# Transposing x of the first problem in ten tiles of 128 tokens instead of four blocks of 320

## The chip, the cores and the metric

The kernel runs on one core of a Trainium2 chip, as one program that drives five engines: TensorE (PE: matmuls; PEld: the weight loads that go with them), VectorE (DVE), ScalarE (ACT), GpSimd (POOL) and SyncE (SP). SP and ACT issue DMAs, each on a queue of its own. The metric is the device time of one execution in microseconds. Before the change the median of five runs is 696.78 us (695.6 to 711.94).

## The reference, cut to what matters

Two problems, A and B, of the same shapes, each a grouped-query attention over a cache, with a projection ahead of it and one behind:

```python
B, Sq, D = 16, 80, 576
Hq, Hkv, Sk, Dh = 32, 16, 512, 128
q = (lambda x, *d: x.transpose(*d))((x @ wq).reshape(B, Sq, Hq, Dh), 0, 2, 1, 3)
k = jnp.repeat(k_cache, rep, axis=1)
v = jnp.repeat(v_cache, rep, axis=1)
scores = jnp.einsum("bhqd,bhkd->bhqk", q, k) * (Dh ** -0.5)
p = _softmax(scores, axis=-1)
o = jnp.einsum("bhqk,bhkd->bhqd", p, v)
return (lambda x, *d: x.transpose(*d))(o, 0, 2, 1, 3).reshape(B, Sq, Hq * Dh) @ wo
```

The results of A and B stand side by side in the last dimension. All tensors are bf16. x of one problem is 16 x 80 = 1280 tokens of 576 values.

## The kernel before, in words

**Units.** The work is cut into 128 units U (problem, group of four K/V heads, batch entry): 64 for A, then 64 for B. A unit has K and V of four heads (512 KB each), its scores (L894: 16 matmuls over 160 columns, two query heads of 80 tokens together), exponentials on ScalarE (L899, three matmuls at a time), and the product with V (L991, L1007). Four units of neighbouring batch entries make a window W with one division by the row sums on VectorE (L1026, L1031), and eight make one output projection (L1050 transposes, L1087 matmuls, L1099 to L1109 sums).

**Queries.** For four batch entries (320 tokens, a block) and eight query heads, a step m of L850 makes q^T: eight jobs `qp` of five matmuls each (L867), one for each 128-row chunk of the 576 rows of x^T and Wq. The fifth chunk takes the last 128 columns of x and meets a Wq chunk whose upper 64 rows are zero. The result is copied to `qT` (L874, by VectorE, or ScalarE for every other head of m = 0). Steps m = 0 to 3 use blocks 0 to 3 of A.

**x^T.** A matmul needs x with its features on the partitions. For B the transposing DMA does that (L773, L776). For A, x is loaded as it lies into the unused accumulator `acc`, and TensorE transposes it (L798) against an identity. Each block of 320 tokens has two loads, of 256 and of 64 tokens (L782, L785), and 15 transposes: for each of the five chunks two of 128 tokens and one of 64. They are put into PSUM in three parts (two chunks, two chunks, one) and copied to `xT` and `xR` (L804: the second part by ScalarE, the others by VectorE). Blocks 0 to 3 use acc rows 2 to 9. The K of units 0 to 3 is also loaded as it lies and transposed on TensorE (L951, L959, L964); from U = 4 on, K comes by the transposing DMA (L927) into five buffers `kT`. K of units 2 and 3 is loaded into acc rows 2 to 5, so its loads wait for the transposes of x blocks 0 and 1 (in the program, after their projections' place in the order). V is loaded (L931) into three buffers and copied by GpSimd into five others with a column of ones beside each head (L934).

**Order.** Every operation is added with an engine and a key; `_Sched.finalize` sorts by key, derives the waits from named resources that are read and written, and each engine runs its operations in that order. Nothing is reordered at run time. The keys are written out by hand in tables: `X_T` for the loads of x, `TX_T` for its transposes (-98, -89, -63, -12), `K_T` and `V_T` for K and V, `W1_T` for the second Wq, `WO_T` for the first Wo, `Q_T` for the early projections; m = 0 stands at -96 + 2i. Jobs on TensorE that go through PSUM take three banks in turn (`JB`, L1134), and the copies that follow them are placed by `place_followers` behind their job's modelled end.

In that order, TensorE begins with eight warm-up matmuls (L752), then the transposes of block 0, four projections, the transposes of block 1 (in front of the fifth projection of m = 0), four projections, the transposes of block 2, and then projections of m = 1 and 2 mixed with the K transposes of unit 0. Scores begin at 31.93 us, and the transposes of block 3 follow the first three of them, at 32.14 us.

**Queues.** SP's queue begins with x of block 0 (two loads), block 2 (two), block 1 (two), V0, K0, K1, V1, x of block 3 (two), K2, V2, K3, V3, and then the transposing K loads with the V loads between them. ACT's queue begins with the first Wq, in three pieces of 256, 256 and 512 columns, each as a load of 512 rows (L822) and one of the last 64 rows (L825), then Wo (L843) and the second Wq (L833).

Of the kernel before, what the change touches and what calls it, by code (L numbers as in the profile page):

```python
# [7 lines left out]
BF16 = mybir.dt.bfloat16  # L8
# [11 lines left out]
NX = 5  # L20
# [598 lines left out]
def bass_concat_heads__gqa_block_cached__gqa_block_cached__near_ridge_kernel(  # L619
# [9 lines left out]
    B, SQ, D = A_x.shape  # L629
# [6 lines left out]
    NSU = 2 * NOCT * B  # L636
    NW = NSU // 4
# [4 lines left out]
    DC = D // 2  # L642
    QN = 4 * SQ
    PVB = (3, 4)
    OKS = 7 % NX
    X_T = (-801.0, -800.0, -800.9, -791.7)
    K_T = (-798.0, -794.0, -60.0, -40.0, 0.0, 3.5, 35.0, 35.5, 59.0, 67.5)
    KVP = (-56.0, -41.0)
    NVS = 20
# [15 lines left out]
    sb = lambda name, shape, dt: fast.enter_context(nc.sbuf_tensor(name, shape, dt))  # L665
    ident = sb("ident", [128, 128], BF16)
    ones = sb("ones", [128, 128], BF16)
    xT = sb("xT", [128, NX, 4, QN], BF16)
    xR = sb("xR", [128, NX, QN], BF16)
    wq_sb = sb("wq_sb", [128, 2, 5, 1024], BF16)  # L670
    qT = sb("qT", [128, NQ, 4, 4, 160], BF16)
    kT = sb("kT", [128, NK, 4, 512], BF16)
# [7 lines left out]
    osb = sb("osb", [128, NOSB, D], BF16)  # L680
    acc = sb("acc", [128, 10, D], F32)
    rinv = sb("rinv", [128, 5 * NSU], F32)
    okm = xT[:, OKS, 0:2, :].rearrange("p a b -> p (a b)")
    warm = acc[:, 0, 0:256].bitcast(BF16)
    okn = sb("okn", [128, 3], F32)
    okb = sb("okb", [128, 1], BF16)
    ps = fast.enter_context(nc.psum_tensor("ps", [128, 8, 512], F32))
    psb = ps[:].bitcast(BF16)
    sem_names = (["e_pe", "e_act", "e_dve", "e_pool"]
                 + ["d_wi%d" % i for i in range(3)] + ["d_wo%d" % i for i in range(2)] + ["d_wq%d" % i for i in range(2)]  # L690
                 + ["d_x%d" % i for i in range(NX)] + ["d_out%d" % i for i in range(NOSB)]
                 + ["d_k%d" % i for i in range(NK)] + ["d_v%d" % i for i in range(NV)])
    sems = {n: nc.alloc_semaphore("f_" + n) for n in sem_names}
# [3 lines left out]
    def R(res, ver):  # L697
        return (res, ver)
# [65 lines left out]
    add("pe", -890, em_warm, reads=[R(("ones",), 0), R(("acc", 0, 0), "warm")], writes=[R(("ps", 0), ("W",))], name="warm")  # L764
    IDENT = R(("ident",), 0)

    for xb in range(8):
        prob, c = divmod(xb, 4)
        x_ap = probs[prob][0].rearrange("b s d -> (b s) d")[c * QN:(c + 1) * QN, :]
        sl = xb % NX  # L770

        def em_ldx(e, x_ap=x_ap, sl=sl):
            return e.dma_start_transpose(xT[:, sl, 0:4, :], x_ap[:, 0:512].rearrange("n (c d) -> n c d", d=128))  # L773

        def em_ldx2(e, x_ap=x_ap, sl=sl):
            return e.dma_start_transpose(xR[:, sl, :], x_ap[:, D - 128:D])  # L776

        if prob == 0:
            xin = acc[:, 2 + 2 * c:4 + 2 * c, :].rearrange("p a d -> p (a d)").bitcast(BF16).rearrange("p (a d) -> p a d", d=D)

            def em_ldz(e, x_ap=x_ap, xin=xin):
                return e.dma_start(xin[:, 0:2, :], x_ap[0:256, :].rearrange("(a p) d -> p a d", p=128))  # L782

            def em_ldzb(e, x_ap=x_ap, xin=xin):
                return e.dma_start(xin[0:64, 2, :], x_ap[256:QN, :])  # L785

            for k_, em in ((0, em_ldz), (1, em_ldzb)):
                add("sp", X_T[c] + 0.1 * k_, em, writes=[R(("acc", 2 + 2 * c + k_, h_), ("x", xb)) for h_ in range(2)],
                    dsem="d_x%d" % sl, name="ldz%d%s" % (xb, "ab"[k_]))
            for part, (k0, k1) in enumerate(((0, 2), (2, 4), (4, 5))):  # L790
                def em_tx(e, bank, k0=k0, k1=k1, xin=xin):
                    last = None
                    for ck in range(k0, k1):
                        d0 = 128 * ck if ck < 4 else D - 128
                        for a in range(3):
                            n = 128 if a < 2 else 64
                            c0 = QN * (ck - k0) + 128 * a
                            last = e.transpose(psb[:, bank, c0:c0 + n], xin[0:n, a, d0:d0 + 128], ident[0:n, 0:n])  # L798
                    return last

                def em_txev(e, bank, k0=k0, k1=k1, sl=sl, part=part):
                    src = psb[:, bank, 0:QN * (k1 - k0)]
                    dst = xT[:, sl, k0:k1, :].rearrange("p a b -> p (a b)") if k0 < 4 else xR[:, sl, :]
                    return e.copy(dst, src) if part == 1 else e.tensor_copy(dst, src)  # L804

                job(TX_T[c] + 0.3 * part, em_tx,
                    [R(("acc", 2 + 2 * c + k_, h_), ("x", xb)) for k_ in range(2) for h_ in range(2)] + [IDENT],
                    "tx%d.%d" % (xb, part), ("X", xb, part),
                    [("act" if part == 1 else "dve", 0.0, em_txev, [], [R(("xT", sl, part), xb)], None)])
            continue  # L810
        t = 16.0 * (36, 46.5, 50, 54)[c] + 9.0
        add("sp", t, em_ldx, writes=[R(("xT", sl, k_), xb) for k_ in range(2)], dsem="d_x%d" % sl, name="ldx%d" % xb)
        add("sp", t + 0.1, em_ldx2, writes=[R(("xT", sl, 2), xb)], dsem="d_x%d" % sl, name="ldx%db" % xb)

    for goct in range(2 * NOCT):
        prob, q = divmod(goct, NOCT)
        wq_ap, wo_ap = probs[prob][3][:, q * 1024:(q + 1) * 1024], probs[prob][4][q * 1024:(q + 1) * 1024, :]
        sl = goct % 2
        if goct == 0:
            for hf, (n0, n1) in enumerate(WQ0):  # L820
                def em_a(e, wq_ap=wq_ap, n0=n0, n1=n1):
                    return e.dma_start(wq_sb[:, 0, 0:4, n0:n1], wq_ap[0:512, n0:n1].rearrange("(c p) n -> p c n", p=128))  # L822

                def em_b(e, wq_ap=wq_ap, n0=n0, n1=n1):
                    return e.dma_start(wq_sb[64:128, 0, 4, n0:n1], wq_ap[512:576, n0:n1])  # L825

                add("act", -799.6 + 0.2 * hf, em_a, writes=[R(("wq", 0, hf, "a"), 0)], dsem="d_wi%d" % hf, name="ldwa0.%d" % hf)
                add("act", -799.5 + 0.2 * hf, em_b, writes=[R(("wq", 0, hf, "b"), 0)], dsem="d_wi%d" % hf, name="ldwb0.%d" % hf)
        else:
            for ck in range(5):  # L830
                def em_w(e, wq_ap=wq_ap, sl=sl, ck=ck):
                    if ck < 4:
                        return e.dma_start(wq_sb[:, sl, ck, :], wq_ap[128 * ck:128 * ck + 128, :])  # L833
                    return e.dma_start(wq_sb[64:128, sl, 4, :], wq_ap[512:576, :])

                wr = [R(("wq", sl, ck), goct)]
                if goct == 2:
                    wr += [R(("wq", 0, hf, ab), 1) for hf in range(3) for ab in "ab"] if ck == 0 else []
                add("act" if goct < 2 else "sp", 256.0 * (goct - 1) + 16.0 + 20.0 * ck if goct > 1 else W1_T[ck], em_w,
                    writes=wr, dsem="d_wq%d" % sl, name="ldw%d.%d" % (goct, ck))  # L840
        for pc in range(4):
            def em_wo(e, wo_ap=wo_ap, sl=sl, pc=pc):
                return e.dma_start(wo_sb[:, sl, 2 * pc:2 * pc + 2, :],  # L843
                                   wo_ap[256 * pc:256 * pc + 256, :].rearrange("(h p) n -> p h n", p=128))

            t = 256.0 * goct - 56.0 + 22.0 * pc
            add("sp" if goct else "act", t if goct else WO_T[pc], em_wo, writes=[R(("wo", sl, pc), goct)], dsem="d_wo%d" % sl,
                name="ldwo%d.%d" % (goct, pc))

    for m in range(2 * NOCT * 4):  # L850
# [4 lines left out]
        for i in range(8):  # L855
# [8 lines left out]
            def em_qp(e, bank, i=i, wsl=wsl, xsl=xsl):  # L864
                last = None
                for ck in range(5):
                    last = e.matmul(ps[:, bank, 0:QN], lhsT=wq_sb[:, wsl, ck, i * 128:(i + 1) * 128],  # L867
                                    rhs=xT[:, xsl, ck, :] if ck < 4 else xR[:, xsl, :], start=(ck == 0), stop=(ck == 4))
                return last

            def em_qev(e, bank, g=g, s_=s_, qsl=qsl, ev=ev):
# [2 lines left out]
                return e.copy(dst, src) if ev == "act" else e.tensor_copy(dst, src)  # L874

            if goct == 0:
                rd = [R(("wq", 0, (0, 0, 1, 1, 2, 2, 2, 2)[i], ab), 0) for ab in "ab"]
            else:
                rd = [R(("wq", wsl, ck), goct) for ck in range(5)]
            job(t, em_qp, rd + [R(("wqz",), 0)] + [R(("xT", xsl, k_), xb) for k_ in range(3)],  # L880
                "qp%d.%d" % (m, i), ("Q", m, i),
                [(ev, t + 2.3, em_qev, [], [R(("qT", qsl, i), m)], None)])

# [35 lines left out]
    for U in range(NSU):  # L919
# [21 lines left out]
        if U < NKP:  # L941
            if U < 2:
                kin = wo_sb[:, 1, 4 * U:4 * U + 4, :].rearrange("p h n -> p (h n)")
                kres = [("wo", 1, 2 * U + k_) for k_ in range(2)]
            else:
                kin = acc[:, 2 * U - 2:2 * U, :].rearrange("p a d -> p (a d)").bitcast(BF16)
                kres = [("acc", 2 * U - 2 + k_, h_) for k_ in range(2) for h_ in range(2)]
            kin = kin[:, 0:2048].rearrange("p (g j d) -> p g j d", g=4, j=4)

            def em_ldy(e, kc_ap=kc_ap, b=b, q=q, kin=kin):  # L950
# [217 lines left out]
        return e.tensor_scalar(flag[:], ps[:, 0, 0:1], 128.0, None, op0=AluOpType.is_equal)  # L1168

    tc = 64.0 * (NW - 1) + 24.0  # L1170
    add("dve", tc, em_c0, reads=[R(("ri", F), 0) for F in range(7 * NW - 7)], writes=[R(("okm", 0), 0), R(("xT", OKS, 0), "chk")], name="chk0")
    add("dve", tc + 0.1, em_c1, reads=[R(("okm", 0), 0)], writes=[R(("okm", 0), 1), R(("okn", 0), 0)], name="chk1")
    add("dve", tc + 0.2, em_rem, reads=[R(("okn", 0), 0)], writes=[R(("okn", 2), 0)], name="chkr")
    tc = 64.0 * (NW - 1) + LAST_T[6] + 0.5
# [102 lines left out]
```

## Time and profile before

| what | value |
|---|---|
| median of the runs | 696.78 us |
| the profiled execution's own time | 694.29 us |
| its span, first to last instruction | 692.5 us |
| VectorE, ScalarE, GpSimd busy | 58%, 55%, 35% of the span |
| transposes of x, L798 | 60, from 5.84 to 33.9 us |
| copies of x^T, L804, VectorE 640 columns / 320 columns | 0.49 us / 0.32 us |
| copies of x^T, L804, ScalarE 640 columns | 0.69 us |
| projections, L867 | 1280 matmuls of 320 columns |
| scores, L894 | 2048 matmuls, first at 31.93 us |
| transposing K loads, L927 | 124, 512 KB each |
| x of A, landed (block 0: two loads) | 4.48 and 5.80 us |
| Wq pieces, landed (rows 0 to 511 / last 64) | 5.22 / 5.99, 7.75 / 10.94, 11.71 / 14.49 us |
| V0, K0, K1, V1, landed | 14.68, 16.76, 18.26, 20.19 us |

The profile is a page for one execution, and a trace behind it that can be asked for parts. Times are counted from the first instruction. A line such as `14.12 1.64 PE ps L798 x15` of the chain of work says: from 14.12 us, for 1.64 us, the chain that ended last ran through 15 matmuls of line 798 that write `ps`. The chain is followed back from the last instruction, at each step to what released it or to the instruction before it on its engine. A busy time counts a matmul from its start to its modelled end, and matmuls overlap; what one costs in a row is the step from one start to the next. Landing times are those of a load's last part.

### The profile page before, as it was taken

Reading aid. Unit: us, or ns where it says so; the run is one execution under the profiler, and the core shown is the slowest. Engines: PE = TensorE matmul, PEld = TensorE weight load, DVE = VectorE, ACT = ScalarE, POOL = GpSimd, SP = SyncE. Lnnn points to the kernel's source line nnn. Section 1 sums busy time; section 2 is a strip of 40 time slices with the busy share of each in tenths; the row PEclk is TensorE's granted clock in tenths of the full one; section 3 lists DMA queues with packets and bytes.
Section 4 is the critical chain, followed back from the end, with each engine's and each line's share of the span. In section 5 each row is a group of like instructions: output and inputs, shape, how many; then the busy total and the mean of one; then the engine's idle time right before and its main releaser. Section 6 shows DMA issues by size and latency. Waiting matters only on the chain.

```text
span 692.5 us, 21462 instructions
## 1 busy us (share of the span) xinstructions
PE 684.0 (99%) x9477; PEld 586.8 (85%) x9477; DVE 398.8 (58%) x1006; ACT 383.8 (55%) x741; POOL 242.2 (35%) x136
## 2 busy tenths in 40 slices
PE   8999999999999999999999999999999999999997
PEld 4788888888888888888888888888888888888885
DVE  1664455565665666666665554555666666656665
ACT  2287666655555555555555666565555555555561
POOL 2314444342244432244423244432244432244430
PEclk9999999999999999999999999999999999999999
DMA  9999999999999999999999999999899988998851
GB/s 265 230 208 218 238 255 247 267 239 246 225 272 246 251 203 268 273 247 229 266 228 258 260 238 225 246 248 222 213 244 236 254 221 197 250 226 206 226 145 40
DMA packets 354297, 160.60 MB, mean 232 GB/s; under 512 B 268568, under 2 KB 350168, under 8 KB 354200
## 3 DMA queue, kind: packets, MB, share of 16 engines
q1 hardware_dynamic: 297536, 103.06, 77.1%
q10 hardware_dynamic: 56664, 56.12, 26.3%
q8 instruction: 75, 1.23, 0.7%
q14 instruction: 22, 0.18, 0.1%
HBM read 89.55 MB, written 2.95 MB: 134 GB/s over the span
## 4 chain that ended last, share of the span: by engine, by line
PE 96%; DMA 1%; DVE 1%; POOL 0%; issue 0%; SPq 0%
PE ps L867 25%; PE ps L1087 22%; PE ps L894 20%; PE ps L991 17%; PE ps L1050 5%; PE ps L1007 5%; PE ps L798 1%; DMA acc<-in_A_x_dram 1%; DMA v_in<-in_A_v_cache_dram 1%; PE ps L959 1%; DVE o_sb L1031 0%; POOL v_sb L934 0%; DVE osb L1109 0%; DVE oM L1057 0%; DVE rinv L1026 0%
## 5 line engine op out<-in xcount | busy, mean ns | idle before, releaser
L899 ACT ACTIVATE P<-ps 128x480 bf16<-128x480 f32 (+1 forms) x683 | 360.2, 571 | 249.6 <-PE ps L894 245.4
L934 POOL COPY v_sb<-v_in 128x2048 bf16<-128x2048 bf16 x128 | 239.6, 1896 | 429.8 <-PE ps L1007 300.5
L894 PE MATMUL ps<-qT,kT 128*128 128x160 bf16 x2048 | 243.5, 232 | 0.0
L991 PE MATMUL ps<-v_sb,P 128*128 128x130 bf16 x2048 | 203.2, 221 | 0.4 <-DVE o_sb L1031 0.4
L874 DVE CAST qT<-ps 128x320 bf16<-128x320 f32 x252 | 131.2, 520 | 113.9 <-PE ps L867 112.4
L867 PE MATMUL ps<-xT,wq_sb 128*128 128x320 bf16 x1024 | 182.5, 301 | 0.4 <-DVE xR L804 0.4
L894 PEld LDWEIGHTS ps<-qT,kT 128*128 128x128 bf16 x2048 | 159.4, 97 | 17.3
L991 PEld LDWEIGHTS ps<-v_sb,P 128*128 128x128 bf16 x2048 | 147.6, 98 | 7.8 <-DVE o_sb L1031 0.6
L1087 PE MATMUL ps<-wo_sb,oM 128*128 128x288 bf16 x1024 | 146.3, 286 | 0.0
L1031 DVE TENSOR_TENSOR o_sb<-ps,rinv 128x384 bf16<-128x384 f32 (+1 forms) x224 | 120.6, 539 | 7.7
L1087 PEld LDWEIGHTS ps<-wo_sb,oM 128*128 128x128 bf16 x1024 | 96.3, 98 | 21.2 <-DMA wo_sb<-in_A_wo_dram 0.2
L867 PEld LDWEIGHTS ps<-xT,wq_sb 128*128 128x128 bf16 x1024 | 92.7, 98 | 23.7 <-DVE xR L804 0.5
L1057 DVE COPY oM<-ps 128x512 bf16<-128x512 bf16 x128 | 54.1, 423 | 47.4 <-PE ps L1050 47.1
L867 PE MATMUL ps<-xR,wq_sb 128*128 128x320 bf16 x256 | 77.1, 301 | 0.0
L1104 DVE TENSOR_TENSOR acc<-ps,acc 128x288 f32<-128x288 f32 x80 | 36.6, 458 | 48.8 <-PE ps L1087 48.8
L1050 PE MATMUL ps<-ident,o_sb 128*128 128x128 bf16 x640 | 60.0, 219 | 0.5 <-DVE o_sb L1031 0.5
L1026 DVE RECIPROCAL rinv<-ps 128x3 f32<-128x3 f32 (+1 forms) x224 | 38.7, 173 | 36.5 <-PE ps L1007 27.0
L1050 PEld LDWEIGHTS ps<-ident,o_sb 128*128 128x128 bf16 x640 | 44.2, 98 | 2.3 <-DVE o_sb L1031 0.7
L1007 PE MATMUL ps<-v_sb,P 128*32 128x130 bf16 x2048 | 36.5, 223 | 0.5 <-DVE o_sb L1031 0.2
L1087 PE MATMUL ps<-wo_sb,oR 128*128 128x288 bf16 x256 | 36.4, 286 | 0.0
L1007 PEld LDWEIGHTS ps<-v_sb,P 128*32 128x32 bf16 x2048 | 30.7, 98 | 5.1 <-DVE o_sb L1031 1.3
L867 PEld LDWEIGHTS ps<-xR,wq_sb 128*128 128x128 bf16 x256 | 25.3, 99 | 10.0
(37 smaller groups left out, 122.2 us busy)
## 6 DMA issues: line engine op xcount, KB each, us to landing
v_in<-in_B_v_cache_dram ACTq DMA_DIRECT2D x64, 512.0 KB, 5.3
v_in<-in_A_v_cache_dram ACTq DMA_DIRECT2D x36, 512.0 KB, 5.6
v_in<-in_A_v_cache_dram SPq DMA_DIRECT2D x28, 512.0 KB, 5.4
wo_sb<-in_B_wo_dram SPq DMA_DIRECT2D x16, 288.0 KB, 5.4
wq_sb<-in_B_wq_dram SPq DMA_DIRECT2D x16, 256.0 KB, 5.6
wo_sb<-in_A_wo_dram SPq DMA_DIRECT2D x12, 288.0 KB, 4.8
out_dram<-osb SPq DMA_DIRECT2D x31, 72.0 KB, 4.1
wq_sb<-in_A_wq_dram SPq DMA_DIRECT2D x8, 256.0 KB, 5.5
```

Source lines behind the costliest of these rows:

```text
L867: last = e.matmul(ps[:, bank, 0:QN], lhsT=wq_sb[:, wsl, ck, i * 128:(i + 1) * 128], rhs=xT[:, xsl, ck, :] if ck < 4 else xR[:, xsl, :], st ...
L874: return e.copy(dst, src) if ev == "act" else e.tensor_copy(dst, src)
L894: last = e.matmul(ps[:, sbk, c * 160:(c + 1) * 160], lhsT=kT[:, U % NK, j, g * 128:(g + 1) * 128], rhs=qT[:, (U // 4) % NQ, U % 4, g, :], ...
L899: return e.activation(P[:, psl, 0:k, :], ps[:, sbk, 0:k * 160].rearrange("p (c n) -> p c n", c=k), AF.Exp, scale=SCALE)
L934: return e.tensor_copy(v_sb[:, vps, :, 0:128], v_in[:, vs, :, :].rearrange("p g (j d) -> p (g j) d", j=4))
L991: last = e.matmul(ps[:, bank, off:off + OP_], lhsT=pap(16 * U + 4 * g + j, 0, 128), rhs=v_sb[:, vps, 4 * g + j, :], start=(j == 0), stop=( ...
L1007: last = e.matmul(ps[32 * g:32 * g + 32, bank, off:off + OP_], lhsT=pap(16 * U + 4 * g + j, 128, 160), rhs=v_sb[:, U % NVP, 4 * g + j, :], ...
L1026: return e.reciprocal(rinv[:, c0:c0 + nt], ps[:, bank, 128:128 + OP_ * (nt - 1) + 1:OP_])
L1031: return e.tensor_tensor(o_sb[:, osl, 0:nt, :], src, sc, AluOpType.mult)
L1050: last = e.transpose(psb[:, bank, 128 * n_:128 * n_ + 128], o_sb[:, F % NOF, pos, :], ident[:])
L1057: return e.tensor_copy(oM[:, osl2, :, 128 * b8:128 * b8 + 128], psb[:, bank, 0:512].rearrange("p (g c) -> p g c", g=4))
L1087: last = e.matmul(ps[:, bank, 0:DC], lhsT=w, rhs=wo_sb[:, wsl, i, ch * DC:(ch + 1) * DC], start=(i == 0), stop=(i == 7))
```

## The change

x of A is no longer cut by block but in ten tiles of 128 tokens, in four groups: tiles 0 to 2, 3 and 4, 5 to 7, 8 and 9. Each group is one load, and 15 or 10 transposes of 128 tokens each. A group of three tiles goes through PSUM in parts of two, two and one chunk; a group of two in parts of three and two chunks; the last part is copied by ScalarE and the others by VectorE. `xT` becomes one tensor with the five chunks outside and all tokens of the slots inside, so a tile may lie across the bound of two blocks; `xR` goes away. `XB` names the groups and parts that each block needs: block 0 needs group 0, block 1 groups 0 and 1, block 2 group 2, block 3 groups 2 and 3.

The keys of the loads change, so that SP's queue begins with group 0, the second piece of Wq (256 columns), group 1, V0, K0, group 2, group 3, K1, V1, K2, V2. ACT's queue begins with the first piece of Wq, then the last 64 rows of all 1024 columns as one load, then the third piece (512 columns). The input tiles take acc rows 2 to 6, and K of units 2 and 3 goes to acc rows 7 and 8, and 0 and 1. The scratch of the final check (`okm`) moves from slot 2 of `xT` to slots 3 and 4 of its first chunk, and B's loads, matmuls and waits name the new layout. The keys of the transposes on TensorE (`TX_T`) and of everything else stay.

```diff
-    OKS = 7 % NX
-    X_T = (-801.0, -800.0, -800.9, -791.7)
+    OKS = 3
+    XG = ((0, 3), (3, 5), (5, 8), (8, 10))
+    XB = (((0, 3),), ((0, 3), (1, 2)), ((2, 3),), ((2, 3), (3, 2)))
+    X_T = (-801.0, -800.0, -796.0, -794.0)
...
-    xT = sb("xT", [128, NX, 4, QN], BF16)
-    xR = sb("xR", [128, NX, QN], BF16)
+    xT = sb("xT", [128, 5, NX * QN], BF16)
...
-    okm = xT[:, OKS, 0:2, :].rearrange("p a b -> p (a b)")
+    okm = xT[:, 0, OKS * QN:OKS * QN + 20 * NSU // 4]
...
-    for xb in range(8):
-        prob, c = divmod(xb, 4)
-        x_ap = probs[prob][0].rearrange("b s d -> (b s) d")[c * QN:(c + 1) * QN, :]
+    xin = acc[:, 2:7, :].rearrange("p a d -> p (a d)").bitcast(BF16).rearrange("p (a d) -> p a d", d=D)
+    xA_ap = probs[0][0].rearrange("b s d -> (b s) d")
+
+    def xres(c):
+        return [("xT", c, g, part) for g, n in XB[c] for part in range(n)]
+
+    for g, (t0, t1) in enumerate(XG):
+        nt = t1 - t0
+
+        def em_ldz(e, t0=t0, t1=t1):
+            return e.dma_start(xin[:, t0:t1, :], xA_ap[128 * t0:128 * t1, :].rearrange("(a p) d -> p a d", p=128))
+
+        xinr = [R(("acc", 2 + t_ // 2, t_ % 2), ("x", g)) for t_ in range(t0, t1)]
+        add("sp", X_T[g], em_ldz, writes=xinr, dsem="d_x%d" % g, name="ldz%d" % g)
+        for part, (k0, k1) in enumerate(((0, 2), (2, 4), (4, 5)) if nt == 3 else ((0, 3), (3, 5))):
+            def em_tx(e, bank, k0=k0, k1=k1, t0=t0, nt=nt):
+                last = None
+                for ck in range(k0, k1):
+                    d0 = 128 * ck if ck < 4 else D - 128
+                    for a in range(nt):
+                        c0 = 128 * (nt * (ck - k0) + a)
+                        last = e.transpose(psb[:, bank, c0:c0 + 128], xin[:, t0 + a, d0:d0 + 128], ident[:])
+                return last
+
+            eng = "act" if part == nt - 1 else "dve"
+
+            def em_txev(e, bank, k0=k0, k1=k1, t0=t0, t1=t1, nt=nt, eng=eng):
+                src = psb[:, bank, 0:128 * nt * (k1 - k0)].rearrange("p (k n) -> p k n", k=k1 - k0)
+                dst = xT[:, k0:k1, 128 * t0:128 * t1]
+                return e.copy(dst, src) if eng == "act" else e.tensor_copy(dst, src)
+
+            job(TX_T[g] + 0.3 * part, em_tx, xinr + [IDENT], "tx%d.%d" % (g, part), ("X", g, part),
+                [(eng, 0.0, em_txev, [], [R(("xT", c, g, part), c) for c in range(4) if (g, len(((0, 2), (2, 4), (4, 5)) if nt == 3 else (0, 0))) in XB[c]], None)])
...
-        if prob == 0:
...
-                add("sp", X_T[c] + 0.1 * k_, em, writes=[R(("acc", 2 + 2 * c + k_, h_), ("x", xb)) for h_ in range(2)],
-                    dsem="d_x%d" % sl, name="ldz%d%s" % (xb, "ab"[k_]))
...
-                add("act", -799.6 + 0.2 * hf, em_a, writes=[R(("wq", 0, hf, "a"), 0)], dsem="d_wi%d" % hf, name="ldwa0.%d" % hf)
-                add("act", -799.5 + 0.2 * hf, em_b, writes=[R(("wq", 0, hf, "b"), 0)], dsem="d_wi%d" % hf, name="ldwb0.%d" % hf)
+                add("sp" if hf == 1 else "act", (-799.6, -800.5, -799.2)[hf], em_a, writes=[R(("wi", hf), 0)],
+                    dsem="d_wi%d" % hf, name="ldwa0.%d" % hf)
+
+            def em_b(e, wq_ap=wq_ap):
+                return e.dma_start(wq_sb[64:128, 0, 4, :], wq_ap[512:576, :])
+
+            add("act", -799.5, em_b, writes=[R(("wi", 3), 0)], dsem="d_wi3", name="ldwb0")
...
-                                    rhs=xT[:, xsl, ck, :] if ck < 4 else xR[:, xsl, :], start=(ck == 0), stop=(ck == 4))
+                                    rhs=xT[:, ck, xsl * QN:(xsl + 1) * QN], start=(ck == 0), stop=(ck == 4))
...
-                rd = [R(("wq", 0, (0, 0, 1, 1, 2, 2, 2, 2)[i], ab), 0) for ab in "ab"]
+                rd = [R(("wi", (0, 0, 1, 1, 2, 2, 2, 2)[i]), 0), R(("wi", 3), 0)]
...
-                kin = acc[:, 2 * U - 2:2 * U, :].rearrange("p a d -> p (a d)").bitcast(BF16)
-                kres = [("acc", 2 * U - 2 + k_, h_) for k_ in range(2) for h_ in range(2)]
+                kin = acc[:, (7, 0)[U - 2]:(9, 2)[U - 2], :].rearrange("p a d -> p (a d)").bitcast(BF16)
+                kres = [("acc", (7, 0)[U - 2] + k_, h_) for k_ in range(2) for h_ in range(2)]
```

## The prediction, made before the changed kernel ran

> **What bounds the kernel now.** I read the page first (busy shares, then the chain of work that ended last), then the chain in order of time for the first 80 us, since all that the change touches for problem A runs in the first 50 us.
>
> ```profile
> PE 684.0 (99%) x9477; PEld 586.8 (85%) x9477; DVE 398.8 (58%) x1006; ACT 383.8 (55%) x741; POOL 242.2 (35%) x136
> ...
> PE 96%; DMA 1%; DVE 1%; POOL 0%; issue 0%; SPq 0%
> ```
>
> TensorE is busy for 99% of the span and holds 96% of the chain, so work taken off TensorE shortens the run, wherever its data are there in time. The chain shows where they are not (start, length, what; the lines are from two stretches):
>
> ```profile
> 1.34 4.46 DMA acc<-in_A_x_dram
> ...
> 5.84 2.54 PE ps L798 x15
> ...
> 8.41 0.34 DVE xR L804
> ...
> 8.79 5.32 PE ps L867 x20
> 14.12 1.64 PE ps L798 x15
> 15.76 2.82 PE ps L867 x20
> 18.58 1.64 PE ps L798 x15
> ...
> 25.08 0.22 PE ps L959 x4
> ...
> 32.30 1.64 PE ps L798 x15
> ```
>
> Three things stand here. The first transposes wait for x until 5.84. The same 20 projection matmuls cost 5.32 us at 8.79 and 2.82 us at 15.76: TensorE steps at half pace (0.267 us a matmul, in the trace's starts) until about 13.6 us, and at 0.136 us after. And a block's 15 transposes (L798) cost 1.64 us, 0.109 each, while the K transposes (L959), each over 128 rows, cost 0.22/4 = 0.055 each. In the starts of the trace it is the 64-row tail that is dear: a full pair steps 0.066 and 0.152, and the step off the tail takes another 0.132.
>
> The second place where TensorE was held is U = 10, the eleventh K/V unit:
>
> ```profile
> 71.56 4.16 DMA v_in<-in_A_v_cache_dram
> ...
> 75.78 1.91 POOL v_sb L934
> ```
>
> V of that unit is issued by SP at 71.56, lands at 75.72, is copied by GpSimd until 77.67, and TensorE's PV starts at 77.73, after 0.3 us of idling. Comparing each unit's landing with its first use, the trace's other narrow places are K at U = 8 and 10 (1.7 and 1.4 us early) and V at U = 8 and 18 (1.4 and 1.1 us early); beyond U = 24, K is over 5 us early throughout. So up to 120 us a TensorE that is earlier gains only what the K/V supply gains too. Its state comes from the table of stretches (stretch, length, busy per engine, clock, DMA share, GB/s):
>
> ```profile
> 26.50:31.50 5.00, 5.00 (x39) 3.62 (x37) 3.71 (x9) 0.00 (x0) 1.67 (x1) 1.00 0.76 53
> 31.50:36.00 4.50, 4.50 (x54) 3.50 (x52) 2.65 (x6) 2.94 (x6) 1.90 (x1) 1.00 1.03 259
> 36.00:38.00 2.00, 2.00 (x24) 1.70 (x23) 1.07 (x3) 1.87 (x5) 0.00 (x0) 1.00 0.00 0
> 38.00:46.00 8.00, 8.00 (x100) 6.93 (x98) 5.11 (x13) 5.63 (x11) 1.90 (x1) 1.00 1.07 280
> 46.00:54.00 8.00, 7.90 (x163) 7.18 (x161) 4.75 (x14) 7.15 (x15) 0.79 (x1) 1.00 1.32 141
> ```
>
> From 36 to 38 us the DMA engines move nothing: SP issues K of U = 5 at 36.76, when TensorE has read the last of U = 0's K (its scores end at 36.59, same buffer). That idling follows TensorE and moves with it. From 38 us the engines are busy, and from 54 to 119 us SP is never without an issue under way. The two thin stretches (53 and 141 GB/s) are where a transposing K load runs beside loads on ACT's queue.
>
> **The change, part by part.** Times are of the profiled execution: span 692.5, its own time 694.29, so 1.8 lie around the span and are left alone. That is 2.5 below the median of the runs shown, 696.78.
>
> *First x load.* Two loads (288 and 72 KB, landed 4.48 and 5.80) become one of 432 KB at the head of SP's queue; the Wq piece of columns 256 to 511 is behind it, not on ACT's queue. Below: 72 KB more than now, by the pace of the x loads behind it (288 KB from 5.80 to 7.01, so 0.3), counted from the 4.86 at which 15 of 16 engines had done the pair, gives 5.2. Above: the third load's 7.01. I take 5.85, as now: more bytes, no short second load, one issue instruction (0.5) less.
>
> *First transposes and copies.* Fifteen full ones at half pace: 15 x 0.110 (twice 0.055) = 1.65 for 2.54 (floor 15 x 0.081, the closest starts of the cold pairs, 1.2). Copies: VectorE took 0.49 for 640 columns and 0.32 for 320, so 0.56 for 768; ScalarE 0.69 for 640 and 0.59 for 512, so 0.48 for 384. VectorE now has two in a row: it starts when six are transposed, 6.6, and ends near 7.75; ScalarE starts at 7.5 and ends near 8.0. The first projection starts at 8.05, not 8.79: 0.74 earlier, but these are half-pace microseconds. If full pace comes at the same 13.6, they are worth 0.37. Wq's first piece landed at 5.22; its rest rows, one load of 128 KB where the first took 32 KB and landed at 5.99, are bounded above by the next column piece's 7.75, still before 8.05.
>
> *Block 1* (tiles 3 and 4): ten transposes, 0.55 for 1.64, less 0.05 for those still at half pace: 1.04. Its load, third on SP, has fewer bytes ahead than the one that landed at 9.87, against a need at 13.4. *Tiles 5 to 7*: fifteen, 0.83 for 1.64; two 768-column copies follow on VectorE with three PSUM banks turning, which may hold TensorE 0.1: 0.71. *Tiles 8 and 9* at 32 us: 0.55 for 1.64: 1.09. The copies beside them lie under projections (0.68 for a group of five, copy 0.52); without that cover each would cost under 0.6.
>
> *Late load.* Tiles 5 to 7 now load behind V0 and K0. Before, K0 landed at 16.76 and K1 at 18.26; by bytes (with its own it has 440 KB less to its end than K1 had, at the 345 GB/s of the stretch from 15 to 18 us) the new load lands near 17.0, and TensorE comes to it at 18.42 - 0.37 - 1.04 = 17.0. Bounds: 15.5 (no wait) to 21.42, the landing of the old x block that stood behind V1. I take 0.2 of waiting, since the byte count is nearest to K1.
>
> *Issues, buffers, waits, layout.* SP issues five loads for eight, with Wq's piece among them, and ACT three for six, at 0.47 to 0.75 each; V0, K0, then the late x loads stand behind, and as all of them wait in a queue that the DMA engines empty until 26 us, fewer issues gain nothing. K of U = 2 and 3 no longer wait for block 0's and 1's projections (SP stood 0.8 at most there, with loads queued): nothing. The chunk-major x^T leaves a matmul's 320 columns contiguous: nothing, bounded either way by the spread of the L867 rows, 0.297 to 0.299 at full pace. The overwriting loads of problem B wait on more names for the same readers, long done. The check's scratch moves to blocks long read: nothing.
>
> Sum on TensorE: 0.37 + 1.04 + 0.71 + 1.09 - 0.2 = 3.0 us earlier from 33 us on.
>
> *What is late next.* U = 5's K can be issued as TensorE frees its buffer, 3.0 earlier, at 33.7, after the K load ahead of it (SP done with that at 31.89, landed 37.12). The 2.0 us hole goes. If the K load ahead still ends near 36, the supply gains 2.0; if that also moves, up to 3.0. At U = 10 the margin is nil, so the run gains what the supply gains there: 2.0 to 3.0, and I take 2.5 (U = 18 has 1.1 to spare).
>
> A rule is weighed here. The Trainium skill, "TensorE: Matmul & The Clock Gate", Part 4 (PE-mode transpose), gives about 275 ns for a 128x128 transpose in a kernel and says that transposes do not count as busy for the clock gate; Part 1 says that the gate opens after a busy window of about 3.4 us whose phase is free. By its 275 ns the ten dropped transposes alone would be 2.75 us; the rows say 0.055 apiece in a stream, so the gain is the tail's, and I go by the rows. Its gate speaks against counting on more: an earlier start may buy only more cold matmuls, which is how 0.74 became 0.37 above.
>
> **Rivals.**
> 1. *Clock earlier.* TensorE's real matmuls start 0.74 sooner and the half pace ends sooner. Half-pace stretch now from 8.79 to 13.6; ending 3 us earlier gives 1.5 more, and if the thin stretch at 26.5 to 31.5 shortens as well the supply follows: gain up to 4.5 to 5. For it: the start. Against: 3.6 us of warm-up matmuls from 1.35 did not change the pace.
> 2. *Swallowed by the supply.* The hole closes, but the K load before it, or U = 6's, takes as much longer because TensorE's lead moves ACT's Wo and Wq loads into it. Gain 0 to 1.3. For it: the margin of nil at U = 10 and the full DMA rows after 38 us.
> 3. *Slower: a third thin stretch.* The transposing load of U = 5 ran alone (two zero microseconds ahead of it). Now it may meet ACT's Wo or Wq loads, as U = 4's and U = 6's did. The 26.5 to 31.5 stretch moved 53 GB/s for 259 after it, so it lost about 5.0 x (1 - 53/259) = 4.0 us. With that loss the supply is 2.5 - 4.0 = 1.5 late at U = 10, and TensorE waits there: +1.5, 695.8 for the profiled execution. It decides from the point where the new loss exceeds the 2.5.
> 4. *The change does not do what it says*, that is, the tail's cost is not its 64 rows and full tiles also step 0.109: then the transposes give only 10 x 0.109 = 1.1 warm and the gain falls to about 1: inside rival 2.
>
> **How the numbers follow.** Forecast 694.29 - 2.5 = 691.8 for a profiled execution; the median stands 2.5 above that execution, so 694.3 is predicted. A difference under 0.2% (1.4 us) is about what a measurement of this kernel cannot tell from none. Chances: forecast 0.55 (gain 1.6 to 3.2: 693.6 to 695.2); rival 1 0.10 (down to 691.8); rivals 2 and 4 0.20 (695.5 to 697.0); rival 3 0.15 (698.2 and more). Faster 0.65, same 0.20, slower 0.15. The range from 691.8 to 697.5 takes in the first three and leaves out most of rival 3.
>
> **What would show it.** Right: L798 with 50 transposes of 128 rows, 0.55 and 0.83 in the chain; the first projection near 8.0; U = 0's scores ending near 33.6; no zero stretch near 36; PV of U = 10 near 75.2. Wrong: a DMA wait at the third L798 group (late load), a 0.267 step past 14 us (clock), more than 0.3 of waiting for v_sb or kT between 55 and 80 us (supply), or a new thin stretch in the GB/s rows.

## The result, and the profile after

The changed kernel takes 702.66 us at the median of 22 runs (before: 697.89, 43 runs beside them, where the five runs shown ahead had 696.78). The ratio is 1.0088, with a 95% interval of [1.0061, 1.0116]: 0.9%, or about 6 us, slower. The prediction was 694.3 us with 0.65 on faster; the time lies above its range. Executions over 1.5% above the fastest of their kernel are left out of every ratio and every "median" below, and as the ones profiled with the result, e2 and e7 (spans 712.3, 717.3 and 709.6) were among them, only their first 100 us are read here, and the waits of SP in e2's; what comes later in the changed kernel is read from a second profile of it, e0_after_again (span 703.6, its own time 705.44).

The page of that second profile, busy shares and chain, to be set against the two lines of before:

```profile
PE 682.0 (97%) x9467; PEld 586.8 (83%) x9467; DVE 398.3 (57%) x1004; ACT 383.5 (55%) x741; POOL 241.9 (34%) x136
...
PE 91%; DMA 6%; DVE 1%; SPq 1%; issue 0%; POOL 0%; ACT 0%; ACTq 0%
```

TensorE has the ten instructions less (9467 for 9477) and is busy about as long, 682.0 us for 684.0. But the chain, which was TensorE's for 96% and DMA's for 1%, now belongs to DMA for 6%. The time did not go into work: TensorE waits for data somewhere. The first question is whether that place is the one that was edited. TensorE by time in the profile taken with the result, from its first real work (start, busy time, group; in brackets the wait ahead of it and its releaser):

```profile
5.49 1.27 PE L789 MATMUL ps<-ident,acc 128*128 128x128 bf16 x15 [0.56 <-DMA acc<-in_A_x_dram]
8.21 2.88 PE L872 MATMUL ps<-xT,wq_sb 128*128 128x320 bf16 x20 [1.46 <-DMA wq_sb<-in_A_wq_dram]
10.93 0.72 PE L789 MATMUL ps<-ident,acc 128*128 128x128 bf16 x10
11.70 2.89 PE L872 MATMUL ps<-xT,wq_sb 128*128 128x320 bf16 x20
```

And its chain in order of time (start, length, what):

```profile
3.82 11.37 DMA acc<-in_A_x_dram
...
15.33 0.51 PE ps L789 x6
...
15.86 0.57 DVE xT L797
...
16.48 0.85 PE ps L872 x5
...
28.41 0.21 PE ps L899 x3
28.62 0.56 PE ps L789 x10
```

The front part is better than forecast. The first 20 projection matmuls cost 2.88 us where before they cost 5.32, and block 0's first scores start at 28.25 for 31.93: TensorE is 3.7 us ahead. Ten transposes cost 0.56, as forecast. Two waits are left: 1.46 for Wq's last rows before the first projection, and 0.74 for group 2's load, on which the chain hangs from 3.82 to 15.19.

So the loss is later. First scores of four K/V units, read from the traces (us; U counts the K/V units, S(U) is the start of the unit's first scores matmul):

| trace | S(0) | S(24) | S(36) | S(64) | S(36) to S(64) | span |
|---|---|---|---|---|---|---|
| before | 31.93 | 144.21 | 205.90 | 351.47 | 145.57 | 692.5 |
| changed kernel, second profile | 28.10 | 140.78 | 202.48 | 362.07 | 159.59 | 703.6 |
| e10, one wait taken out (below) | 28.24 | 140.76 | 202.47 | 348.04 | 145.57 | 689.2 |

Until U = 36 most of the lead is kept: 3.4 us. Between U = 36 and 64 the changed kernel spends 159.59 - 145.57 = 14.0 us more than before. In that stretch the transposing loads of x of problem B stand on SP's queue. The queue by time (start, time of the issue, line, what), first one place of it in the trace of before, then two in the second profile:

```profile
266.18 2.56 SPq L773 DMA_TRANSPOSE xT<-in_B_x_dram  x1
268.77 1.25 SPq L776 DMA_TRANSPOSE xR<-in_B_x_dram  x1
270.07 3.72 SPq L927 DMA_TRANSPOSE kT<-in_A_k_cache_dram  x1
```

```profile
263.38 2.13 SPq L808 DMA_TRANSPOSE xT<-in_B_x_dram  x1
270.40 1.13 SPq L811 DMA_TRANSPOSE xT<-in_B_x_dram  x1
271.57 3.08 SPq L932 DMA_TRANSPOSE kT<-in_A_k_cache_dram  x1
...
289.64 1.50 SPq L808 DMA_TRANSPOSE xT<-in_B_x_dram  x1
296.94 1.14 SPq L811 DMA_TRANSPOSE xT<-in_B_x_dram  x1
298.13 4.08 SPq L932 DMA_TRANSPOSE kT<-in_A_k_cache_dram  x1
```

The waits of SP from 255 to 345 us in the second profile (engine, line, waited for: us in total, times, longest):

```profile
SPq L811 <- DMA xT<-in_B_x_dram: 14.5, 3, 5.8
```

L808 loads chunks 0 to 3 of a block's x^T and L811 chunk 4 (before: L773 and L776). In the trace of before the second follows the first at once. Now it waits 4.9, 5.8 and 3.8 us, each time until the first has landed, and the K loads behind it on the queue wait too. TensorE from 290 to 350 us in the same trace, first by its waits:

```profile
PE ps L899 <- DMA kT<-in_A_k_cache_dram: 9.9, 3, 4.3
```

then by the stretch of 300 to 350 us (length, busy per engine, clock, DMA share, GB/s), before and now:

```profile
300.00:350.00 50.00, 50.00 (x686) 43.47 (x684) 30.19 (x75) 27.38 (x52) 17.03 (x10) 1.00 1.19 250
300.00:350.00 50.00, 40.09 (x523) 33.54 (x522) 22.27 (x56) 19.34 (x37) 10.91 (x7) 0.90 1.08 194
```

TensorE idles 9.9 us for K, in waits of 2.3, 3.3 and 4.3 us, and the clock column reads 0.90: the granted clock is 0.5 for 3.4 us from 323.2 and for 6.8 us from 336.8. In those stretches TensorE works for some 7.5 us, from the end of the second wait (323.64) to 326.6 and from the end of the third (339.05) to 343.6, at half pace (0.267 us a projection matmul). Work of 7.5 us at half pace costs some 3.7 us; the 14.0 less the 9.9 leaves about 4.

The reason stands in the code. Both loads of a pair are given the names of what they overwrite:

```python
add("sp", t, em_ldx, writes=[R(("xT", sl, "B", 0), xb)] + ([R(r_, xb) for r_ in xres(sl)] if sl < 4 else []), ...)
add("sp", t + 0.1, em_ldx2, writes=[R(("xT", sl, "B", 1), xb)] + ([R(r_, xb) for r_ in xres(sl)] if sl < 4 else []), ...)
```

`finalize` makes a writer of a name wait for the name's last writer, so the second load is released by the landing of the first, though they write different chunks. Before, the pair's second load named only `("xT", sl, 2)`, which the first does not write.

### The profile page after: what moved, and what is told of

Same layout as the page of the kernel before. It is cut to its first block, busy times and chain, and to the rows that moved or that the text cites. A ratio compares the mean times of both kernels' runs of the same rounds, so it can differ in the third digit from the quotient of the medians.

```text
span 712.3 us, 21435 instructions
## 1 busy us (share of the span) xinstructions
PE 682.8 (96%) x9467; PEld 586.4 (82%) x9467; DVE 398.5 (56%) x1004; ACT 383.8 (54%) x741; POOL 242.0 (34%) x136
## 4 chain that ended last, share of the span: by engine, by line
PE 84%; DMA 13%; DVE 1%; issue 1%; SPq 0%; POOL 0%; ACT 0%; ACTq 0%
PE ps L872 22%; PE ps L1092 20%; PE ps L899 18%; PE ps L996 15%; DMA kT<-in_A_k_cache_dram 8%; PE ps L1055 5%; PE ps L1012 4%; DMA kT<-in_B_k_cache_dram 2%; DMA acc<-in_A_x_dram 2%; DMA v_in<-in_A_v_cache_dram 1%; PE ps L964 1%; DVE o_sb L1036 0%; POOL v_sb L939 0%; DVE osb L1114 0%; DVE oM L1062 0%
## 5 line engine op out<-in xcount | busy, mean ns | idle before, releaser
L872 PE MATMUL ps<-xT,wq_sb 128*128 128x320 bf16 x1280 | 214.1, 300 | 1.7 <-DMA wq_sb<-in_A_wq_dram 1.5
L872 PEld LDWEIGHTS ps<-xT,wq_sb 128*128 128x128 bf16 x1280 | 117.5, 98 | 34.4 <-ACT xT L797 1.6
L1109 DVE TENSOR_TENSOR acc<-ps,acc 128x288 f32<-128x288 f32 x80 | 36.6, 458 | 52.6 <-PE ps L1092 52.6
L1114 DVE TENSOR_TENSOR osb<-ps,acc 128x288 bf16<-128x288 f32 x40 | 18.3, 457 | 29.4 <-PE ps L1092 22.6
L1104 ACT COPY acc<-ps 128x288 f32<-128x288 f32 x40 | 16.0, 399 | 24.7 <-PE ps L1092 24.5
```

## The experiments

**Theory WAIT**: this order between the two loads is the loss. **Rival FRONT**: the tiles, or the new order of the first loads, do harm, in the supply or on the queues (rivals 2 and 3 of the prediction). **Rival LATE** (LEAD in the expectations): the loss comes from an earlier TensorE that meets a DMA system no faster. **Rival LAYOUT**: the new layout of `xT` makes B's transposing x loads themselves slow. Within WAIT there are two ways to price it: every microsecond that SP stands costs one (SUM; PRICE in the expectation of e4), or it costs only what is left when the lead of K over its use, from its landing to the unit's first scores, is gone (SLACK).

**e0_after_again: the changed kernel once more**, beside the others on one chip.

> The changed kernel again, for a trace. In the first trace of it the second x load of three of B's blocks (to slots 0, 1 and 2) names the same resources as the first and so waits on SP until the first has landed: 3.6 to 5.9 us each, with the K loads behind. Theory WAIT: that wait costs the time; expected here: the same three gaps on SP, K of U = 52 to 62 landing late, TensorE waiting for kT after them, a ratio near 1.009. Theory LEAD: TensorE is 3.5 us earlier at 33 us and its lead moves loads into the transposing K loads; expected: thin DMA stretches and waits for kT or v_sb before 200 us, far from the pairs. Theory LAYOUT: the strided destination makes B's transposing x loads themselves slow; expected: landing times of these loads well over the 4.8 and 5.0 us that they took before.

Measured: 1.0048 [0.997, 1.0127], median 704.97. The interval holds the expected 1.009 and also 1.000, so by itself this run does not tell the kernel from before. It gives the profile read above, with the three gaps on SP and no wait for kT ahead of them, and the base for e1, on the same chip.

**e1_no_pair_wait: the order taken out.** The first load still waits for what it overwrites, and the second follows it on the queue.

```diff
-        add("sp", t + 0.1, em_ldx2, writes=[R(("xT", sl, "B", 1), xb)] + ([R(r_, xb) for r_ in xres(sl)] if sl < 4 else []), ...)
+        add("sp", t + 0.1, em_ldx2, writes=[R(("xT", sl, "B", 1), xb)], ...)
```

> The changed kernel with one edit: the second load of each pair no longer names the resources of A's block, so it no longer waits for the first of its pair. WAIT: the loss goes and TensorE's 3 us show: ratio about 0.995 to 0.997 to the kernel before, no idle SP between the loads of a pair. LEAD and LAYOUT: still about 1.009.

Measured: 0.9894 [0.9823, 0.9965], median 695.96: 9.0 us below e0 on the same chip (its slowest run counted, 700.18, is below e0's fastest, 704.07), and faster than before, by more than the expected 0.995 to 0.997. Its trace has no SP wait on `xT`. The tiles, the new first loads and the early TensorE (S(0) at 28.18) are all still in it, so FRONT and LATE do not account for the loss. One caution: this trace still waited 3.7 us for kT once, after a stretch in which DMA moved 205 GB/s (190 to 230 us; 255 in the trace of before). It was run twice more:

> The run without pair waits once more, as what the other three are compared with on this chip: 0.990 to 0.997 of the kernel before.

> The run without the pair wait, for the comparison with the other two on this chip: 0.993 to 0.997 of the kernel before.

Measured: 0.9894 [0.9821, 0.9967], and 0.9982 [0.9938, 1.0026]. All three are below the 1.0088 of the changed kernel; how far below before, the third leaves open. The third's trace is the cleanest. Its queue at the same place:

```profile
263.27 1.43 SPq L808 DMA_TRANSPOSE xT<-in_B_x_dram  x1
264.75 1.95 SPq L811 DMA_TRANSPOSE xT<-in_B_x_dram  x1
266.74 4.13 SPq L932 DMA_TRANSPOSE kT<-in_A_k_cache_dram  x1
```

and its stretch of 300 to 350 us:

```profile
300.00:350.00 50.00, 50.00 (x685) 43.45 (x683) 30.97 (x77) 27.02 (x52) 16.81 (x9) 1.00 1.19 248
```

The second load goes out at 264.75 for 270.40, and the next K load at 266.74 for 271.57. TensorE is busy for all 50 us (40.09 with the waits), at 1.00, and DMA moves 248 GB/s for 194. From S(36) to S(64) it takes 145.57 us, to the digit what before took. The layout is still the new one, and the first loads of the three pairs land 5.9, 4.9 and 6.2 us after their issue, for 6.0, 4.9 and 8.0 before: LAYOUT is not seen.

**e2_before_plus_wait: the order put into the kernel before**, with nothing else of the change.

```diff
-        add("sp", t + 0.1, em_ldx2, writes=[R(("xT", sl, 2), xb)], ...)
+        add("sp", t + 0.1, em_ldx2, writes=[R(("xT", sl, 2), xb)] + ([R(("xT", sl, 0), xb)] if sl < 4 else []), ...)
```

> The kernel before with one edit: the second load of the pairs to slots 0, 1 and 2 waits for the first to land; nothing else of the change. WAIT: slower by 6 to 10 us (the changed kernel lost 6 net while being some 3 earlier at the start): ratio 1.009 to 1.014. LEAD and LAYOUT: ratio 1.000, as neither a lead nor a layout is in it.

Measured: 1.0094 [1.0015, 1.0173]. SP's waits from 255 to 345 us:

```profile
SPq L776 <- DMA xT<-in_B_x_dram: 15.3, 3, 6.4
```

The same three waits appear without tiles and without the new first loads, and so does the loss. Neither FRONT nor LATE is needed for it.

**e3_tiles_alone: the tiles without the new order of Wq** (keys as before, and Wq's six loads on ACT; without the pair's order).

```diff
-    X_T = (-801.0, -800.0, -796.0, -794.0)
+    X_T = (-801.0, -800.0, -800.9, -791.7)
...
-                add("sp" if hf == 1 else "act", (-799.6, -800.5, -799.2)[hf], em_a, writes=[R(("wi", hf), 0)], ...)
-            add("act", -799.5, em_b, writes=[R(("wi", 3), 0)], dsem="d_wi3", name="ldwb0")
+                add("act", -799.6 + 0.2 * hf, em_a, writes=[R(("wq", 0, hf, "a"), 0)], ...)
+                add("act", -799.5 + 0.2 * hf, em_b, writes=[R(("wq", 0, hf, "b"), 0)], ...)
```

> As the run without the pair wait, but Wq's first loads all six on ACT's queue as before, and the x groups at the old keys (group 2 ahead of group 1, group 3 behind V1): the ten tiles without the new queue order. By the terms of the prediction the tiles give 0.37 + 1.04 + 0.71 + 1.09 = 3.2 on TensorE by 33 us, and the order of the loads nothing but a late group 2 (0.2): ratio 0.995 to 0.997, within 0.001 of the run without the pair wait. If the order of the loads matters, they differ by more.

Measured: 0.990 [0.983, 0.997]; S(0) at 29.76 for 28.18 in e1. TensorE's waits in the first 30 us:

```profile
PE ps L870 <- DMA wq_sb<-in_A_wq_dram: 4.2, 3, 1.7
```

Tiles alone make TensorE early enough to wait for Wq's pieces (the last landed at 14.0). By these two traces the new order is worth 1.6 us of lead at U = 0; the runs' times do not tell the two apart. This trace, too, waits for kT without any pair wait, 5.9 us in all, at U = 57 to 60, and takes 154.41 us from S(36) to S(64).

**e8_wq_order_alone: the other half**, before with only the new Wq loads (the reverse of the lines above; x keys as before).

> The kernel before with only the new Wq loads (second piece on SP, the last 64 rows in one load); x stays in four blocks. In the run of the tiles with the old Wq order TensorE waited 4.2 us for Wq, in three waits, as the last rows' third load landed at 14.1; in the kernel before it came to that piece at 15.7, so it had nothing to wait for. So the new order alone is expected to give nothing: 0.998 to 1.002. If it removes a hidden cost by itself: 0.997 or less.

Measured: 1.0001 [0.9963, 1.004]; S(0) at 31.55 for 31.93. By itself the new order is worth nothing measurable: before, TensorE was not waiting for Wq.

**e4_one_pair_waits: the order kept for the first pair alone**, which tells SUM from SLACK.

```diff
-... + ([R(r_, xb) for r_ in xres(sl)] if sl < 4 else []), dsem="d_x%d" % sl, name="ldx%db" % xb)
+... + ([R(r_, xb) for r_ in xres(sl)] if xb == 5 else []), dsem="d_x%d" % sl, name="ldx%db" % xb)
```

> The changed kernel with the pair wait left in one of the three pairs only (the first, block 5, near 265 us; U = 48 has K 14 us ahead there). Theory SLACK (each wait stops SP for 4 to 6 us, K's lead of 10 to 14 us hides one, three within 65 us add up): K's lead dips by about 5 and TensorE does not wait for it; time within 1.5 us of the run without pair waits. Theory PRICE (each wait costs its own length whatever the lead): 3 to 5 us slower than the run without.

Measured: 0.9935 [0.9906, 0.9965]. SP's waits:

```profile
SPq L811 <- DMA xT<-in_B_x_dram: 4.5, 1, 4.5
```

K's lead over its use falls from 12.5 us (U = 51) to 10.7 (U = 52), hardly more than in e10 without any wait (12.7 to 11.3), and TensorE does not wait there. The median is 691.48, 0.8 us above the 690.64 of e7 on the same chip, where SLACK expected at most 1.5 and PRICE 3 to 5; that speaks for SLACK, though the two intervals overlap. The trace itself is not clean: it waits 5.7 us for kT elsewhere, at U = 42 and 43, ahead of the pair, and at U = 59 and 60, some 60 us behind it. DMA was slower than before in both stretches (215 GB/s for 255 from 190 to 230 us, 239 for 266 from 260 to 300).

In e0 the leads follow the same account: 14.5 us at U = 48, then 6.6 (U = 52), 2.2 (U = 56) and 0.1 to 1.0 from U = 57 to 60, where TensorE stalls. Before, they are 11 to 16 us from U = 48 to 59, and 7.0 at U = 60.

**e5_wait_behind_k: the order kept, its place moved**, so that a K load stands between the two.

```diff
-        add("sp", t + 0.1, em_ldx2, ...)
+        add("sp", t + 20.0, em_ldx2, ...)
```

> The changed kernel, all three waits left in, but the second load of a pair given a key 20 later, so that one or two K loads and a Wq or Wo load stand between the two. By the time SP comes to the wait the first load has landed or nearly so. WAIT and its place: as the run without pair waits, within 1 us. If it is not the wait on SP but the second load itself, or the dependency as such, that costs: still 8 us slower than that run.

Measured: 0.9944 [0.9895, 0.9994]. SP's queue:

```profile
262.77 1.55 SPq L808 DMA_TRANSPOSE xT<-in_B_x_dram  x1
265.01 3.83 SPq L932 DMA_TRANSPOSE kT<-in_A_k_cache_dram  x1
...
274.32 1.24 SPq L811 DMA_TRANSPOSE xT<-in_B_x_dram  x1
```

K goes out between the two, the first x load has landed when the second's turn comes, and no SP wait on `xT` is left, though both still write the same names. S(36) to S(64) is 145.9, span 689.7. So it is not the dependency that costs, but what is queued behind it while it waits. The "within 1 us" of the expectation is not resolved: the medians differ by 3.9 (694.56 and 690.64 of e7), the intervals overlap.

**e6_group2_first: a better version**, e1 with group 2's load ahead of V0 and K0, and Wq's last rows in two halves, since those are the two waits left in front.

```diff
-    X_T = (-801.0, -800.0, -796.0, -794.0)
+    X_T = (-801.0, -800.0, -799.0, -794.0)
...
-                return e.dma_start(wq_sb[64:128, 0, 4, :], wq_ap[512:576, :])
-            add("act", -799.5, em_b, writes=[R(("wi", 3), 0)], ...)
+                return e.dma_start(wq_sb[64:128, 0, 4, n0:n1], wq_ap[512:576, n0:n1])
+                add("act", (-799.5, -799.1)[hf], em_b, writes=[R(("wi", 3 + hf), 0)], ...)
```

> Without the pair wait, and with the two waits gone that the changed kernel's trace shows in its first 16 us: group 2 of x loads ahead of V0 and K0 (TensorE waited 1.0 us for it at 14.4), and Wq's rest rows in two loads of 512 columns (the first projection waited for all 1024 columns' rows until 8.0, some 1.5 us). TensorE up to 2 us earlier at the first scores (26.5 to 27.5 for 28.2). At V of U = 10 and 18 the run without pair waits has 1 to 2 us to spare, so 0.5 to 1.5 us of it reach the end: 0.998 to 0.9995 of that run. If the K/V supply has no room left: the same time.

> The run without the pair wait, with group 2 ahead of V0 and Wq's last rows in two loads, once more: first scores near 27.1 us, 0.5 to 1.5 us less than the run without the pair wait on the same chip, 0.991 to 0.995 of the kernel before.

Measured: 0.9926 [0.9882, 0.997] and 0.9928 [0.9889, 0.9967], medians 689.71 and 691.64. The chain of e6 at the start:

```profile
11.31 2.88 PE ps L873 x20
14.19 0.96 PE ps L789 x15
```

The group 2 transposes now follow block 1's projections at once: the wait of 0.74 is gone and S(0) is at 26.95, another 1.3 us earlier. The second run of this version misses the expected 27.1: its S(0) is at 28.44, as TensorE fell back to half pace from 7.7 to 11.1 us. Both intervals lie below 1, so this version beats the kernel before, and the changed kernel's 1.0088 with it. Whether it also beats e1 is not settled: it is 0.9 and 2.4 us below by the medians of the runs on the same chips (e7 and e10), for an expected 0.5 to 1.5.

## Why the prediction was wrong

**The step that failed** is one sentence of "Issues, buffers, waits, layout": "The overwriting loads of problem B wait on more names for the same readers, long done." The readers are long done, but the names have writers as well: the first load of the pair writes every one of the names of A's block that the second overwrites. The dependency was priced at nothing. In e0's trace it stood SP up three times (14.5 us in all), and TensorE lost 14.0 us between U = 36 and 64; by the runs it is worth 9.0 us (e1 against e0) and 0.9% (e2 against before). The place is far from what I looked at, some 230 us behind it, in lines that the change only renamed. e1, e2 and e5 show it from three sides: with the wait out the loss is gone; with the wait put into before it is there; with a K load in between it is gone again.

The sum follows: TensorE was 3.4 us ahead at U = 36, lost 14.0, which leaves it 10.6 late; the spans differ by 11.1 (703.6 for 692.5). Not all of the 14.0 need be the wait's. K of U = 58 goes out 10.1 us later than in e10 (308.11 for 297.98), which the queue explains, but then also takes 15.4 us to land for 9.7. And traces without any pair wait can lose in the same stretch: it took 150.90 us in e1 and 154.41 in e3.

**Point by point, on the rest.**

- *First x load, first projection.* Forecast 8.05, measured 7.92 to 8.21 (the two profiles of the changed kernel, e1 and e10), for another reason than given. The transposes began at 5.4 to 5.5, earlier than the 5.85 taken, and in three of the four ran at full pace for a part or nearly all; then TensorE waited 0.9 to 1.7 us for Wq's rest rows, which landed at 7.7 to 8.0. They were bounded by 7.75, and they were the last thing in.
- *Half pace until 13.6* was wrong, and is the largest term of the front. In the changed kernel full pace comes at 6.1 and 5.8 (two profiles). That is rival 1, and with the shorter transposes it made block 1's projections 4.1 us early (11.55 in e10 for 15.69). Some of it ends at the late load, where TensorE waits till 15.2. At U = 0 3.7 are left, where the terms ahead of it give 1.9; with tiles 8 and 9, which follow, it is 4.8 (U = 0's scores end at 31.8 for 36.6), where 3.0 were forecast. The Trainium skill ("TensorE: Matmul & The Clock Gate", Part 1) calls the phase of the gate's window free; the same eight warm-up matmuls, begun at 1.35 us, were followed by full pace anywhere from 4.3 to 13.8 us in these traces, which agrees.
- *Transposes.* 0.055 to 0.056 apiece at full pace, ten in 0.56, as forecast; rival 4, that full tiles would step 0.109 too, did not happen. The skill's Part 4 figure of about 275 ns for one in a kernel is five times what they cost in a stream here; it is nearer to the busy time of a single one, 0.219 us from start to modelled end at full pace (L964 in e10). So the choice of the row held.
- *Late load.* Taken as 0.2 of waiting with a landing near 17.0. It landed at 15.2, and TensorE, earlier, waited 0.74 to 0.88. (The stretch from 15 to 18 us moved 348 GB/s, not 345, which changes nothing.) Group 2 then cost 1.15 from its first transpose to the first projection, for 0.83 + 0.1: a VectorE copy (0.57) stands on the chain.
- *Supply.* Forecast: of the 3.0 on TensorE 2.0 to 3.0 come through, 2.5 taken. Measured: of the 4.8, 3.4. The hole from 36 to 38 us is filled, as forecast; but TensorE, earlier, now idles some 1.5 us between 46 and 54 us, where it was busy for 7.90 of the 8 us before. In e10:

```profile
36.00:38.00 2.00, 2.00 (x24) 1.66 (x22) 1.38 (x4) 1.34 (x4) 0.00 (x0) 1.00 0.80 263
46.00:54.00 8.00, 6.54 (x132) 5.50 (x130) 3.52 (x11) 4.93 (x11) 3.73 (x2) 1.00 1.35 178
```

  The PV of U = 10 starts at 74.09 in the profile taken with the result, for 77.73 (forecast 75.2).
- *Rivals.* Rival 2 happened in part, as the 1.4 us show; in e9's trace, after a wait of 2.6 us near 50 us and 3.4 us at half pace, only 0.3 of 4.6 us of lead are left at U = 10. Rival 3 had the right sign by the wrong mechanism: in the second profile of the changed kernel no wait for K came before U = 57, behind the second pair.

With the front alone the spans of e10 and before give a gain of 3.3 (0.5%), where 2.5 was forecast; the ratios of 0.9894, 0.9894 and 0.9982 lie around it. That the two are so near is in part luck: TensorE gained 1.8 us more than forecast, and the supply took 1.4 where 0.5 was taken.

**Open.** Whether the tiles cause the earlier full pace: with tiles eight of ten traces have it from 5.1 to 7.1 on, for all of the front, and two opened (4.3, 5.0) and fell back until 11.1 and 11.8; without tiles three have 13.8, 12.7, and 5.1 with a fall-back from 8.5 to 11.9. Denser transposes ahead of it would fit, but no run changed that alone. Some of the gain does not hang on it: with the fall-back, too, S(0) is at 28.44 and 28.96 with tiles, for 30.41 without. Also open is why DMA moves 40 to 50 GB/s less for tens of microseconds in some traces (e1, e4), which let TensorE wait for kT where no pair had waited, and why K comes late in e3.

## What to carry to other kernels

When one load becomes the writer of a name that another load on the same queue also writes, ask what orders the two: give the overwritten names to one of them, or to each its own part. By e4 and e5 a wait on an issuing queue is not priced by its length but by the lead of what is queued behind it, and waits that come faster than the lead recovers add up: one of 4.5 us made 0.8 us by the medians, three of 14.5 us together 9.0. When a tensor is renamed or its layout is cut anew, go through the waits of every operation that names it, those far from the edit too.

## What the runs showed of the hardware

- A TensorE wait can cost more than itself. Waits of 2.6 us (e4, e9), 3.7 (e1), and 3.3 and 4.3 (e0) each went with a granted clock of 0.5 for 3.4 us, or 6.8 with the last; a wait of 2.3 us did so in e3 and not in e0, and one of 2.1 us in e5 did not.
- The clock row does not show the half pace of the start: in the trace of before it reads 1.00 from 8 to 12 us, where the projections step 0.267 us. It does show a fall-back (0.50 from 8 to 10 us in e9). The steps between starts are the safer reading.
- A transposing load of x on SP holds the second of a pair for 3.8 to 5.8 us (e0) if that has to wait for its landing, while its issue alone takes 1.1 to 2.6 us (before, e0 and e10).
